# Threshold attention with a feed-forward block: TensorE in program order, feed-forward assigned to the next batch's blocks, two score buffers in the first batch, weights from SyncE's queue

## The chip, the cores and the metric

One core of one Trainium2 chip. The metric is the device time of one execution in microseconds (us), median of several runs. The program uses a single core, so there is no second die to look at; runs of a kernel agree within 0.1 to 0.7% here.

## The reference, cut to what matters

```python
# 8 batches, 8 heads, 576 tokens, head size 64, all float32 (weights come as float64)
scores = (q @ k.T) / 8
scores = where(scores >= max(scores) - tau, scores, -1e9)     # tau = 0.02
attn   = exp(scores - max(scores)); attn /= attn.sum() + 1e-9
x      = (attn @ v) with heads side by side      # 4608 tokens x 512
out    = relu(x @ w_in)**2 @ w_out               # 512 -> 2048 -> 512
```

## The kernel before

Two heads of 64 form a pair that fills the 128 rows of TensorE: 4 pairs per batch, 32 in all. A pair has five blocks of queries (four of 128 rows, one of 64). Each block goes through scores (TensorE), maximum (VectorE), exponential (ScalarE), mask with row sums (VectorE), nine transposes (TensorE; five in the block of 64). After its last block a pair's values are multiplied and divided by the sums. The feed-forward runs on 18 pieces of 256 tokens: 8 hidden groups of 8 matmuls of 256 columns, then 2 x 16 output matmuls of 512 columns.

PSUM has eight banks. One score tile takes four, and four single banks serve everything else:

```python
sc = ps.tile([P, 4 * BANK], FP32, tag="sc", bufs=1, name="sc")     # one score buffer
def bank(shape, name): return ps.tile(shape, FP32, tag="b", name=name)   # bufs=4
```

The feed-forward is cut into units that the loop over blocks hands out evenly; the scheduler may reorder each engine's instructions:

```python
per_slot = NPIECE * 16 / len(slots)
for n in range(len(slots) + 1):
    if n < len(slots): sc = scores(*slots[n])
    if n > 0:          transposes(*slots[n - 1])
    if n < len(slots): softmax(*slots[n], sc)
    ...                                        # cut: next pair's q and k, values
    weights_until(min(2 * (n + 1), len(chunks)))
    credit = run(credit + per_slot) if todo else 0.0
```

In the first batch it takes two blocks of all four pairs first, so that 256 tokens are ready early, and multiplies their values in two halves. Weights are fetched from GpSimd's DMA queue and converted from float64 by ScalarE, VectorE and GpSimd.

## Time and profile before

| | before |
|---|---|
| median of 3 runs | 1737.53 us (1736.78 to 1739.94) |
| span of the profiled run | 1732.0 us, mean granted TensorE clock 0.977 |
| TensorE busy | 1643.5 us, 95% |
| VectorE, ScalarE, GpSimd busy | 33%, 34%, 16% |

TensorE is the bound, and its few holes lie in the first 90 us and around 300 to 370 us. The lines, and how each is read, stand in the prediction. One more view: what TensorE waited for, with the total in us, how often, and the longest wait.

```profile
PE pwT L258 <- DVE w L237: 41.7, 14, 5.0
PE sc L211 <- DVE w L237: 14.6, 7, 2.4
```

Transposes waiting for the mask, 42 us in 14 waits, are the largest item in the whole run of 1732 us.

### The profile page before, as it was taken

Reading aid. Unit: us, or ns where it says so; the run is one execution under the profiler, and the core shown is the slowest. Engines: PE = TensorE matmul, PEld = TensorE weight load, DVE = VectorE, ACT = ScalarE, POOL = GpSimd, SP = SyncE. Lnnn points to the kernel's source line nnn. Section 1 sums busy time; section 2 is a strip of 40 time slices with the busy share of each in tenths; the row PEclk is TensorE's granted clock in tenths of the full one; section 3 lists DMA queues with packets and bytes.
Section 4 is the critical chain, followed back from the end, with each engine's and each line's share of the span. In section 5 each row is a group of like instructions: output and inputs, shape, how many; then the busy total and the mean of one; then the engine's idle time right before and its main releaser. Section 6 shows DMA issues by size and latency. Waiting matters only on the chain.

```text
span 1732.0 us, 19750 instructions
## 1 busy us (share of the span) xinstructions
PE 1643.5 (95%) x7720; PEld 1038.6 (60%) x7720; DVE 569.2 (33%) x1218; ACT 581.8 (34%) x1241; POOL 271.4 (16%) x322
## 2 busy tenths in 40 slices
PE   5699899699999999989999999999999999999998
PEld 3474564366564747566666666565756575747764
DVE  4745333433333333333333333333333333320000
ACT  4644333333333323233333333332333332321100
POOL 4654010001010201011011011010101010102210
PEclk9799999889998999999999999999999999999999
DMA  7532101000101010010101010101010000000000
GB/s 197 165 97 81 34 21 33 21 22 22 33 15 33 21 27 16 24 27 21 34 17 30 22 33 7 34 21 34 15 33 21 19 15 13 1 12 0 13 12 12
DMA packets 128108, 56.70 MB, mean 33 GB/s; under 512 B 121616, under 2 KB 121616, under 8 KB 128016
## 3 DMA queue, kind: packets, MB, share of 16 engines
q1 hardware_dynamic: 120528, 29.22, 7.6%
q0 software_dynamic: 7488, 26.22, 4.5%
q8 instruction: 62, 1.02, 0.2%
q14 instruction: 30, 0.25, 0.1%
HBM read 45.97 MB, written 9.44 MB: 32 GB/s over the span
## 4 chain that ended last, share of the span: by engine, by line
PE 87%; ACT 4%; DVE 3%; issue 3%; POOL 2%; DMA 1%; SPq 0%; POOLq 0%; ACTq 0%
PE ph L334 29%; PE po L352 26%; PE sc L211 12%; PE pwT L258 7%; PE pv L291 7%; PE pqk L180 1%; ACT w L233 1%; PE pv L285 1%; DVE w L237 1%; PE pwT L263 1%; PE pr L309 1%; ACT wT L265 1%; PE pwR L268 1%; DVE nmx L225 1%; DVE t L118 1%
## 5 line engine op out<-in xcount | busy, mean ns | idle before, releaser
L334 PE MATMUL ph<-x,w_in 128*128 128x256 f32 x2304 | 514.4, 381 | 4.5 <-ACT rb L310 2.8
L352 PE MATMUL po<-w_out,g 128*128 128x512 f32 x1152 | 510.8, 593 | 1.4 <-POOL w_out L123 1.4
L334 PEld LDWEIGHTS ph<-x,w_in 128*128 128x128 f32 x2304 | 433.2, 190 | 74.0 <-ACT rb L317 9.1
L225 DVE TENSOR_REDUCE nmx<-sc 128x2 f32<-128x1152 f32 (+1 forms) x160 | 197.9, 1237 | 633.8 <-PE sc L211 633.8
L352 PEld LDWEIGHTS po<-w_out,g 128*128 128x128 f32 x1152 | 212.5, 190 | 232.6 <-issue 228.1
L237 DVE SCALAR_TENSOR_TENSOR w<-sc,thr,w 128x576 f32<-128x576 f32 x288 | 225.2, 815 | 186.7 <-ACT w L233 186.6
L211 PE MATMUL sc<-kT,qT 64*128 64x64 f32 (+3 forms) x1280 | 235.7, 466 | 15.7 <-DVE w L237 14.6
L259 ACT COPY wT<-pwT 128x512 f32<-128x512 f32 x256 | 138.8, 588 | 320.8 <-PE pwT L258 320.5
L340 POOL TENSOR_TENSOR g<-h 128x512 f32<-128x512 f32 x144 | 149.7, 1039 | 563.7 <-ACT h L338 563.7
L211 PEld LDWEIGHTS sc<-kT,qT 64*128 64x128 f32 (+1 forms) x1280 | 115.0, 187 | 185.5 <-issue 181.4
L338 ACT ACTIVATE h<-ph 128x512 f32<-128x512 f32 x144 | 86.0, 597 | 363.7 <-PE ph L334 337.6
L233 ACT ACTIVATE w<-sc,nmx 128x576 f32<-128x576 f32 x288 | 202.0, 756 | 8.6 <-DVE nmx L225 7.7
L258 PE MATMUL pwT<-ident,w 128*128 128x128 f32 x1024 | 151.0, 290 | 42.1 <-DVE w L237 41.7
L258 PEld LDWEIGHTS pwT<-ident,w 128*128 128x128 f32 x1024 | 114.1, 145 | 55.1 <-DVE w L237 39.3
L291 PE MATMUL pv<-wT,va 128*64 128x64 f32 (+2 forms) x1088 | 136.9, 400 | 0.0
L357 POOL DMA_DIRECT2D out_dram<-o x36 | 20.2, 561 | 574.0 <-ACT o L356 574.0
L291 PEld LDWEIGHTS pv<-wT,va 128*64 128x64 f32 x1088 | 60.2, 138 | 73.9 <-issue 68.2
L356 ACT COPY o<-po 128x512 f32<-128x512 f32 x36 | 21.1, 585 | 189.3 <-PE po L352 189.3
L302 POOL COPY rx<-rcp 128x512 f32<-128x512 f32 (+1 forms) x36 | 21.6, 600 | 264.7 <-DVE rcp L300 264.7
L325 DVE TENSOR_TENSOR x<-pv,rb 128x64 f32<-128x64 f32 (+3 forms) x120 | 31.3, 312 | 93.5 <-ACT rb L310 93.2
L310 ACT COPY rb<-pr 128x512 f32<-128x512 f32 (+1 forms) x36 | 19.4, 540 | 116.1 <-PE pr L309 116.1
L265 ACT COPY wT<-pwT 128x256 f32<-128x256 f32 x64 | 20.7, 375 | 105.9 <-PE pwT L263 105.9
(47 smaller groups left out, 698.0 us busy)
## 6 DMA issues: line engine op xcount, KB each, us to landing
out_dram<-o POOLq DMA_DIRECT2D x36, 256.0 KB, 2.3
qn<-in_q_dram SPq DMA_DIRECT2D x66, 128.0 KB, 2.5
kn<-in_k_dram SPq DMA_DIRECT2D x66, 128.0 KB, 2.7
va<-in_v_dram SPq DMA_DIRECT2D x66, 128.0 KB, 2.9
raw<-in_moe_w_in_dram POOLq DMA_DIRECT2D x16, 512.0 KB, 5.1
raw<-in_moe_w_out_dram POOLq DMA_DIRECT2D x16, 512.0 KB, 4.2
rn<-in_q_dram SPq DMA_DIRECT2D x66, 16.0 KB, 2.4
rn<-in_k_dram SPq DMA_DIRECT2D x66, 16.0 KB, 2.5
```

Of the source, the lines that this page charges most:

```text
L211: nc.tensor.matmul(to, qT[rows, ds(t * P, m)], kT[rows, ds(k0, n)], start=True, stop=True)
L225: nc.vector.tensor_reduce(out=nmx[:, 0:nj], in_=every, axis=AXIS.X, op=ALU.max, negate=True)
L233: nc.scalar.activation(out=w[:, ts(j, S)], in_=sc[:, ds(at[j], S)], func=AF.Exp, bias=nmx[:, j : j + 1], scale=1.0)
L237: nc.vector.scalar_tensor_tensor(out=w[:, ts(j, S)], in0=sc[:, ds(at[j], S)], scalar=thr[:, j : j + 1], in1=w[:, ts(j, S)], op0=ALU.is_ge, ...
L258: nc.tensor.transpose(pt[:, c, :], w[:, ds(j * (S + REST) + c * P, P)], ident[:, :])
L259: nc.scalar.copy(wT[:, j, :, ts(t, P)], pt[:, :, :])
L265: nc.scalar.copy(wT[:, j, :, rest], pt[:, :, ds(j * REST, REST)])
L291: nc.tensor.matmul(to[rows, :], va[:, c, rows], wT[:, j, c, ds(q0, n)], start=False, stop=(c == FULL - 1), skip_group_check=True,)
L334: nc.tensor.matmul(ph[:, m, :], w_in[:, c, ts(f + m, P)], x[:, c, :], start=(c == 0), stop=(c == NP - 1))
L338: nc.scalar.activation(out=h[:, :, :], in_=ph[:, :, :], func=AF.Relu)
L340: nc.gpsimd.tensor_mul(g[:, :, :], h[:, :, :], h[:, :, :])
L352: nc.tensor.matmul(po[:, :], gT[f][:, ts(s, P)], w_out[:, f, :], start=(f == 0), stop=(f == NF - 1))
```

## The change

Its intent: keep TensorE full with work placed by hand. TensorE's instructions stay in program order. The first batch, which has no feed-forward to mix in, is taken whole with two score buffers of three banks, so that the next block's scores are made before this block's transposes. From the second batch on, the feed-forward of one batch is spread over the twenty blocks of the next, by a budget in us. Smaller parts: the values of the first batch in one piece; the rest keys of a first-batch block as one matmul over a diagonal tile; fewer, larger loads of q, k and v; weights from SyncE's queue, and converted at 1.25 chunks per block, not two.

```diff
-    ps = ctx.enter_context(tc.tile_pool(name="ps", bufs=4, space=...PSUM))
+    def open_psum(stack, n_scores, bufs, n_banks): ...      # cut
-        nc.gpsimd.dma_start(out=raw[:, :], in_=src.bitcast(I32))
+        nc.sync.dma_start(out=raw[:, :], in_=src.bitcast(I32))
...
+    def feed_forward(x, piece):
+        for f in range(0, NF, 2):                 # NF = 16: eight groups
+            for m in range(2):
+                for c in range(NP):               # NP = 4
+                    nc.tensor.matmul(ph[:, m, :], ...)
+                    ... yield 0.44
+        for s in range(PT // P):
+            for f in range(NF):
+                nc.tensor.matmul(po[:, :], ...)
+                ... yield 0.87
+
+    PIECE = 16 * 8 * 0.44 + 2 * 16 * 0.87
...
+    def run(us):
+        while todo and us > 0:
+            step = next(todo[0], None)
+            if step is None: todo.popleft()
+            else: us -= step; asked["us"] -= step
+        return us
+    share = [0.5] + [4.5 / (NB - 1)] * (NB - 1)
...
+    with ExitStack() as stack, tc.manual_schedule(engines={mybir.EngineType.PE}):
+        open_psum(stack, 3, 2, 2)                 # first batch: two score buffers
+        ...                                       # begin(n + 1) before end(n)
+    with ExitStack() as stack, tc.manual_schedule(engines={mybir.EngineType.PE}):
+        open_psum(stack, 4, 1, 4)                 # the others: one
+        late = 0.0
+        for n in range(n_first, len(slots)):
+            convert_for(n)
+            begin(n)                              # scores, softmax, last pair's values
+            if n % n_first == 0: per_slot = asked["us"] / n_first
+            late = run(per_slot * share[t] + late)
+            end(n)                                # transposes
```

More of the change, by code (lines that the diff above doesn't have):

```diff
@@ L55, with open_psum @@
     sb = ctx.enter_context(tc.tile_pool(name="sb", bufs=2))
-    ps = ctx.enter_context(tc.tile_pool(name="ps", bufs=4, space=bass.MemoryType.PSUM))
+    PSUM = bass.MemoryType.PSUM
+    psum = {}
+    def open_psum(stack, n_scores, bufs, n_banks):
+        psum["n"] = n_scores
+        psum["sc"] = stack.enter_context(tc.tile_pool(name=f"sc{n_scores}", bufs=bufs, space=PSUM))
+        psum["b"] = stack.enter_context(tc.tile_pool(name=f"b{n_banks}", bufs=n_banks, space=PSUM))
     def bank(shape, name):
-        return ps.tile(shape, FP32, tag="b", name=name)
+        return psum["b"].tile(shape, FP32, tag="b", name=name)
     ident = const.tile([P, P], FP32, name="ident")
@@ L78 @@
     vdiag = [const.tile([P, P], FP32, name=f"vdiag{i}") for i in range(4)]
-    for t in vdiag:
+    kdiag = [const.tile([P, P], FP32, name=f"kdiag{i}") for i in range(2)]
+    for t in vdiag + kdiag:
         nc.gpsimd.memset(t[:, :], 0.0)
@@ L88, in fetch_weight @@
         if src.dtype == FP32:
-            nc.gpsimd.dma_start(out=dst, in_=src)
+            nc.sync.dma_start(out=dst, in_=src)
             return None
         raw = sb.tile([P, 2 * WC], I32, tag="raw", bufs=3, name="raw")
-        nc.gpsimd.dma_start(out=raw[:, :], in_=src.bitcast(I32))
+        nc.sync.dma_start(out=raw[:, :], in_=src.bitcast(I32))
         return raw
@@ L154, in load @@
         b, hp = pairs[i]
+        h = 2 * hp
         qn = sb.tile([P, FULL, P], FP32, tag="qn", name="qn")
         kn = sb.tile([P, FULL, P], FP32, tag="kn", name="kn")
-        va = sb.tile([P, FULL, P], FP32, tag="va", bufs=4, name="va")
+        va = sb.tile([P, 2, FULL, D], FP32, tag="va", bufs=3, name="va")
         rn = sb.tile([P, P], FP32, tag="rn", name="rn")
         vd = vdiag[i % 4]
-        for src, dst, order, rest in (
-            (q, qn, "(t p) d -> p t d", lambda j: rn[0:REST, ds(j * D, D)]),
-            (k, kn, "(p t) d -> p t d", lambda j: rn[REST:P, ds(j * D, D)]),
-            (v, va, "(p t) d -> p t d", lambda j: vd[ds(j * D, D), ds(j * D, D)]),
-        ):
-            for j in range(2):
-                h = 2 * hp + j
-                nc.sync.dma_start(out=dst[:, :, ds(j * D, D)], in_=src[b, h, 0:MAIN, :].rearrange(order, p=P))
-                nc.sync.dma_start(out=rest(j), in_=src[b, h, MAIN:S, :])
+        for src, dst, order, rows in ((q, qn, "(t p) d -> p t d", 0), (k, kn, "(p t) d -> p t d", REST)):
+            for j in range(2):
+                nc.sync.dma_start(out=dst[:, :, ds(j * D, D)], in_=src[b, h + j, 0:MAIN, :].rearrange(order, p=P))
+            nc.sync.dma_start(
+                out=rn[ds(rows, REST), :].rearrange("p (j d) -> p j d", j=2),
+                in_=src[b, h : h + 2, MAIN:S, :].rearrange("j p d -> p j d"),
+            )
+        nc.sync.dma_start(out=va[:, :, :, :], in_=v[b, h : h + 2, 0:MAIN, :].rearrange("j (p t) d -> p j t d", p=P))
+        for j in range(2):
+            nc.sync.dma_start(out=vd[ds(j * D, D), ds(j * D, D)], in_=v[b, h + j, MAIN:S, :])
         loaded[i] = (qn, kn, rn, va, vd)
@@ L174, in turn @@
         qn, kn, rn, va, vd = loaded.pop(i)
-        qT = sb.tile([P, S], FP32, tag="qT", bufs=4, name="qT")
-        kT = sb.tile([P, S], FP32, tag="kT", bufs=4, name="kT")
+        qT = sb.tile([P, S], FP32, tag="qT", name="qT")
+        kT = sb.tile([P, S], FP32, tag="kT", name="kT")
         for nat, to in ((qn, qT), (kn, kT)):
@@ L189, in turn @@
         nc.scalar.copy(kT[:, MAIN:S], pt[:, REST:P])
+        if pairs[i][0] == 0:
+            for j in range(2):
+                rows = ds(j * D, D)
+                nc.gpsimd.tensor_copy(out=kdiag[i % 2][rows, ds(j * REST, REST)], in_=kT[rows, MAIN:S])
         turned[i] = (qT, kT, va, vd)
@@ L198, in scores @@
         m = BLK[t]
-        sc = ps.tile([P, 4 * BANK], FP32, tag="sc", bufs=1, name="sc")
-        for part in range(2):
+        n_banks = psum["n"]
+        sc = psum["sc"].tile([P, n_banks * BANK], FP32, tag="sc", name="sc")
+        b_main = (n_banks - 1) * BANK
+        one_rest = t < FULL and n_banks == 3
+        for part in range(1 if one_rest else 2):
             for j in range(2):
@@ L209, in scores @@
                 else:
-                    to = sc[:, ds((3 * BANK, 3 * BANK - REST)[part], n)]
+                    to = sc[:, ds((b_main, b_main - REST)[part], n)]
                 nc.tensor.matmul(to, qT[rows, ds(t * P, m)], kT[rows, ds(k0, n)], start=True, stop=True)
+        if one_rest:
+            to = sc[:, MAIN:S]
+            to = bass.AP(tensor=to.tensor, offset=to.offset, ap=[to.ap[0], [b_main - S, 2], [1, REST]])
+            nc.tensor.matmul(to, qT[:, ts(t, P)], kdiag[i % 2][:, :], start=True, stop=True)
         return sc
@@ L216, in softmax @@
         nj = 2 if t < FULL else 1
-        at = (0, 3 * BANK - REST)[0:nj]
+        at = (0, (psum["n"] - 1) * BANK - REST)[0:nj]
         if i not in sums:
@@ L274, in transposes, with values, reciprocals @@
                 nc.scalar.copy(wR[rows, rest], pt[rows, ds(j * REST, REST)])
-    def values(i, t0, t1):
+    def values(i):
         b, hp = pairs[i]
         wT, wR = weights.pop(i)
-        _, _, va, vd = turned[i]
-        nt = min(t1, FULL) - t0
-        parts = [(t0 * P, nt * P)] + ([(MAIN, REST)] if t1 == NB else [])
+        _, _, va, vd = turned.pop(i)
+        sm = sums.pop(i)
+        last = 2 * FULL
+        rcp = sb.tile([P, 2 * NB], FP32, tag="rcp", name="rcp")
+        nc.vector.tensor_scalar(
+            out=rcp[:, 0 : last + 1], in0=sm[:, 0 : last + 1], scalar1=1e-9, scalar2=None, op0=ALU.add
+        )
+        nc.vector.reciprocal(out=rcp[:, 0 : last + 1], in_=rcp[:, 0 : last + 1])
+        rx = sb.tile([P, FULL, 2, D], FP32, tag="rx", bufs=1, name="rx")
+        nc.gpsimd.tensor_copy(
+            out=rx.rearrange("p t j d -> p (t j) d"), in_=rcp[:, 0:last].unsqueeze(2).broadcast_to([P, last, D])
+        )
+        rb = sb.tile([P, S], FP32, tag="rb", name="rb")
+        yield
+        def reciprocals():
+            pr = bank([P, FULL, P], "pr")
+            for t in range(FULL):
+                nc.tensor.transpose(pr[:, t, :], rx[:, t, :, :].rearrange("p j d -> p (j d)"), ident[:, :])
+            nc.scalar.copy(rb[:, 0:MAIN], pr.rearrange("p t m -> p (t m)"))
+            pr = bank([P, P], "prr")
+            nc.tensor.transpose(pr[:, :], rcp[:, last : last + 1].broadcast_to([P, P]), ident[:, :])
+            for j in range(2):
+                rows = ds(j * REST, REST)
+                nc.scalar.copy(rb[rows, MAIN:S], pr[rows, ds(j * REST, REST)])
+        if b == 0:
+            reciprocals()
+        parts = [(0, MAIN), (MAIN, REST)]
         pv = [bank([P, n], "pv") for _, n in parts]
@@ L291, in values @@
                     nc.tensor.matmul(
-                        to[rows, :], va[:, c, rows], wT[:, j, c, ds(q0, n)], start=False, stop=(c == FULL - 1),
+                        to[rows, :], va[:, j, c, :], wT[:, j, c, ds(q0, n)], start=False, stop=(c == FULL - 1),
                         skip_group_check=True,
                     )
-        sm = sums.pop(i)
-        s0, s1 = 2 * t0, min(2 * t1, 2 * FULL + 1)
-        rcp = sb.tile([P, 2 * NB], FP32, tag="rcp", name="rcp")
-        nc.vector.tensor_scalar(out=rcp[:, s0:s1], in0=sm[:, s0:s1], scalar1=1e-9, scalar2=None, op0=ALU.add)
-        nc.vector.reciprocal(out=rcp[:, s0:s1], in_=rcp[:, s0:s1])
-        rx = sb.tile([P, FULL, 2, D], FP32, tag="rx", bufs=1, name="rx")
-        nc.gpsimd.tensor_copy(
-            out=rx[:, 0:nt, :, :].rearrange("p t j d -> p (t j) d"),
-            in_=rcp[:, s0 : s0 + 2 * nt].unsqueeze(2).broadcast_to([P, 2 * nt, D]),
-        )
-        rb = sb.tile([P, S], FP32, tag="rb", name="rb")
-        pr = bank([P, FULL, P], "pr")
-        for t in range(nt):
-            nc.tensor.transpose(pr[:, t, :], rx[:, t, :, :].rearrange("p j d -> p (j d)"), ident[:, :])
-        nc.scalar.copy(rb[:, ds(t0 * P, nt * P)], pr[:, 0:nt, :].rearrange("p t m -> p (t m)"))
-        if t1 == NB:
-            turned.pop(i)
-            pr = bank([P, P], "prr")
-            nc.tensor.transpose(pr[:, :], rcp[:, 2 * FULL : 2 * FULL + 1].broadcast_to([P, P]), ident[:, :])
-            for j in range(2):
-                rows = ds(j * REST, REST)
-                nc.scalar.copy(rb[rows, MAIN:S], pr[rows, ds(j * REST, REST)])
+        if b > 0:
+            reciprocals()
         for (q0, n), to in zip(parts, pv):
@@ L326, in values @@
                 at += step
-    def hidden(x, gT, f):
-        def go():
+    def feed_forward(x, piece):
+        gT = {}
+        for f in range(0, NF, 2):
             weights_until(NP * (f * P // WC + 1))
@@ L336, in go @@
                     )
+                    if (m, c) != (1, NP - 1):
+                        yield 0.44
             h = sb.tile([P, 2, PT], FP32, tag="h", name="h")
@@ L341, in go @@
             gT[f], gT[f + 1] = g[:, 0, :], g[:, 1, :]
-        return go
-    def output(gT, row, s, f0, f1):
-        def go():
-            weights_until(n_in + f1)
-            if f0 == 0:
-                gT[s, "po"] = bank([P, DM], "po")
-            po = gT[s, "po"]
-            for f in range(f0, f1):
+            yield 0.44
+        for s in range(PT // P):
+            po = bank([P, DM], "po")
+            for f in range(NF):
+                weights_until(n_in + f + 1)
                 nc.tensor.matmul(po[:, :], gT[f][:, ts(s, P)], w_out[:, f, :], start=(f == 0), stop=(f == NF - 1))
-            if f1 < NF:
-                return
+                if f < NF - 1:
+                    yield 0.87
             o = sb.tile([P, DM], FP32, tag="o", name="o")
             nc.scalar.copy(o[:, :], po[:, :])
-            nc.gpsimd.dma_start(out=out[ds(row, P), :], in_=o[:, :])
-        return go
+            nc.gpsimd.dma_start(out=out[ds(piece * PT + s * P, P), :], in_=o[:, :])
+            yield 0.87
+    PIECE = 16 * 8 * 0.44 + 2 * 16 * 0.87
     todo = deque()
-    asked = {"pieces": 0}
+    asked = {"pieces": 0, "us": 0.0}
     def feed_forward_until(tokens):
@@ L367, in feed_forward_until @@
             piece = asked["pieces"]
-            x, gT = xs.pop(piece), {}
-            for f in range(0, NF, 2):
-                todo.append(hidden(x, gT, f))
-            for s in range(PT // P):
-                for f in range(0, NF, 4):
-                    todo.append(output(gT, piece * PT + s * P, s, f, f + 4))
-            asked["pieces"] = piece + 1
-    def run(units):
-        while todo and units >= 1:
-            todo.popleft()()
-            units -= 1
-        return units
-    HALF = 2
@@ L384 @@
-    slots = [(i, t) for i in range(NP) for t in range(HALF)]
-    slots += [(i, t) for i in range(NP) for t in range(HALF, NB)]
-    slots += [(i, t) for i in range(NP, len(pairs)) for t in range(NB)]
-    ends = {}
-    for i in range(len(pairs)):
-        if i < NP:
-            ends[i, HALF - 1] = (0, HALF)
-            ends[i, NB - 1] = (HALF, NB)
-        else:
-            ends[i, NB - 1] = (0, NB)
-    per_slot = NPIECE * 16 / len(slots)
-    load(0)
-    load(1)
-    turn(0)
-    weights_until(1)
@@ L400 @@
-    credit = 0.0
-    for n in range(len(slots) + 1):
-        if n < len(slots):
-            sc = scores(*slots[n])
-        if n > 0:
-            transposes(*slots[n - 1])
-        if n < len(slots):
-            softmax(*slots[n], sc)
-            i, t = slots[n]
-            if (t == 0 and i + 1 < NP) or (t == NB - 2 and NP <= i + 1 < len(pairs)):
-                turn(i + 1)
-                if i + 2 < NP or (NP < i + 2 < len(pairs)):
-                    load(i + 2)
-        if n > 0 and slots[n - 1] in ends:
-            i, t = slots[n - 1]
-            values(i, *ends[i, t])
-            if i == 0 and t == NB - 1:
-                load(NP)
-            if i == 1 and t == NB - 1:
-                load(NP + 1)
-            b, hp = pairs[i]
-            if hp == NP - 1:
-                feed_forward_until(b * S + (MAIN if t == NB - 1 else P * HALF) + (REST if t == NB - 1 else 0))
-        weights_until(min(2 * (n + 1), len(chunks)))
-        credit = run(credit + per_slot) if todo else 0.0
@@ L426 @@
-    run(float("inf"))
+            todo.append(feed_forward(xs.pop(piece), piece))
+            asked["pieces"] = piece + 1
+            asked["us"] += PIECE
+    def run(us):
+        while todo and us > 0:
+            step = next(todo[0], None)
+            if step is None:
+                todo.popleft()
+            else:
+                us -= step
+                asked["us"] -= step
+        return us
+    slots = [(i, t) for i in range(len(pairs)) for t in range(NB)]
+    n_first = NP * NB
@@ new lines, with begin, end @@
+    share = [0.5] + [4.5 / (NB - 1)] * (NB - 1)
+    due = deque()
+    def begin(n):
+        i, t = slots[n]
+        softmax(i, t, scores(i, t))
+        if due:
+            for _ in due.popleft():
+                pass
+            b, hp = pairs[i - 1]
+            if hp == NP - 1:
+                feed_forward_until((b + 1) * S)
+        if t == NB - 2 and i + 1 < len(pairs):
+            turn(i + 1)
+            if i + 2 < len(pairs):
+                load(i + 2)
+    def end(n):
+        i, t = slots[n]
+        transposes(i, t)
+        if t == NB - 1:
+            job = values(i)
+            next(job)
+            due.append(job)
@@ new lines, in convert_for @@
+    def convert_for(n):
+        weights_until(min((5 * (n + 1)) // 4, len(chunks)))
+    with ExitStack() as stack, tc.manual_schedule(engines={mybir.EngineType.PE}):
+        open_psum(stack, 3, 2, 2)
+        load(0)
+        load(1)
+        turn(0)
+        begin(0)
+        for n in range(n_first):
+            convert_for(n)
+            if n + 1 < n_first:
+                begin(n + 1)
+            end(n)
[3 more added lines that the diff above has]
+        for n in range(n_first, len(slots)):
+            t = slots[n][1]
+            convert_for(n)
+            begin(n)
+            if n % n_first == 0:
+                per_slot = asked["us"] / n_first
+            late = run(per_slot * share[t] + late)
+            end(n)
+        for _ in due.popleft():
+            pass
+        feed_forward_until(B * S)
+        run(float("inf"))
```

## The prediction

> **What bounds the kernel now.** I read the page first (shares and 40 slices), then the groups by line, then TensorE's own order of time, then the chain of waits around the one stretch where TensorE is not full.
>
> ```profile
> span 1732.0 us, 19750 instructions
> PE 1643.5 (95%) x7720; PEld 1038.6 (60%) x7720; DVE 569.2 (33%) x1218; ACT 581.8 (34%) x1241; POOL 271.4 (16%) x322
> PE   5699899699999999989999999999999999999998
> ...
> PEclk9799999889998999999999999999999999999999
> ...
> L334 PE MATMUL ph<-x,w_in 128*128 128x256 f32 x2304 | 514.4, 381 | 4.5 <-ACT rb L310 2.8
> L352 PE MATMUL po<-w_out,g 128*128 128x512 f32 x1152 | 510.8, 593 | 1.4 <-POOL w_out L123 1.4
> ```
>
> TensorE is busy 95% of the span, and from the tenth slice on nearly without a hole: it is the bound. Each fp32 matmul of the source has two records, so the feed-forward is 514.4 + 510.8 = 1025 us of it, or 57 us for each of the 18 pieces of 256 tokens. The other 618 us are attention: 32 pairs of heads with five blocks each. The scheduler mixes feed-forward into the attention so that TensorE has work while VectorE and ScalarE do the softmax. One stretch shows what a block costs when there is none to mix in, about 300 to 370 us, seventh to ninth slice:
>
> ```profile
> 303.10:346.40 43.30, 28.11 (x151) 16.97 (x152) 20.98 (x45) 16.99 (x37) 0.61 (x1) 0.83 0.09 21
> 1558.80:1602.10 43.30, 43.30 (x165) 31.27 (x165) 0.74 (x4) 5.44 (x10) 8.89 (x9) 1.00 0.00 0
> ```
>
> These are windows: stretch, length, then busy time of TensorE, its weight loads, VectorE, ScalarE, GpSimd, then the granted clock. The attention-only stretch has TensorE busy 28 of 43 us at clock 0.83; the second, feed-forward alone, is 43.3 of 43.3 at 1.00. The chain of waits inside the first, start and length:
>
> ```profile
> 305.50 2.35 PE sc L211 x8
> 307.86 0.02 issue
> 307.88 1.37 DVE nmx L225
> 309.25 0.02 issue
> 309.27 1.38 ACT w L233 x2
> 310.65 0.03 issue
> 310.68 0.84 DVE w L237 x2
> 311.51 0.05 issue
> 311.56 1.12 PE pwT L258 x4
> 312.68 2.21 PE sc L211 x8
> 314.88 0.60 PE pwT L258 x4
> ```
>
> Scores, maximum, exponentials, mask, transposes: one after the other, since there is a single score buffer. From the end of the scores (307.85) to the first transpose (311.56) TensorE stands 3.7 us. A pair takes 34.3 us here (scores starting at 298.98 and at 333.30), the next one 37.3 (to 370.55); hidden under feed-forward it would take about 18.
>
> **What the Trainium skill says.** (1) "TensorE: Matmul & The Clock Gate", Part 1: the clock is halved after a window of 3413 ns with the engine idle and restored after a busy one; windows run freely. The trace agrees: transposes of four records take 1.12 us after the 3.0 us gaps and 0.66 us when warm, scores 2.4 against 1.3, and the returns to full speed (307.8, 314.8, 342.0) lie about whole multiples of 3.41 us apart. A mostly idle window was enough. (2) Same page, Part 2 ("What happens when you issue a matmul"): matmuls stay in program order, only weight loads are pulled ahead. So an exposed wait in TensorE's program order is not filled by the hardware. (3) "Perfetto Trace Analysis", Identifying Performance Opportunities: equal bubbles again and again can mean too little PSUM for the next tile. That is the 3.7 us above. (4) "DMA: Bandwidth & Descriptors", Issuing engines are not separate DMA queues: another issuing engine only saves its own issue time. In the trace the 32 weight issues take 9.6 + 9.4 = 19 us of GpSimd, which is 16% busy.
>
> **The change part by part.** I built the changed kernel (not run) and read TensorE's instruction order, since a fixed order is the main thing here.
>
> 1. *Values of the first four pairs whole instead of in two halves.* Before: 16 source matmuls of 256 columns per pair, 32 records at 19.5 us / 128 = 0.152 us busy each; after: 8 of 512, 16 records at 102.5 / 448 = 0.229. 4.9 against 3.7 us, four pairs: about 5 us less work.
> 2. *Rest keys of the first batch as one matmul of 128 columns over a diagonal tile*: two of 64 wide go, 16 blocks; by 52.0 us / 256 = 0.20 us each, at most 3 us.
> 3. *First batch, two three-bank score buffers.* No feed-forward exists yet. In VectorE's built order each block has maximum 1.36, threshold 0.23, two masks 1.57, and conversions at 0.48 + 0.84 us for 1.25 weight chunks; next block's maximum mostly follows this block's masks. Masks also wait for the exponentials, 1.4 us. I take 5.2 us x 16 = 83; four 64-row blocks at 3.5 = 14; copies and products 7; about 3 us at each of three value products (two spare banks, all taken) = 9; start 16.5 (first maximum was at 17.06 before). Sum 130 us until the second batch starts.
> 4. *Feed-forward "spread over the next batch".* The budget of a piece is 16*8*0.44 + 2*16*0.87 = 84 us. But the loop goes over f in steps of two: 8 groups x 8 matmuls = 64 steps of 0.44, so a piece really spends 28.2 + 27.8 = 56 us. Two pieces therefore end after 112 / 8.4 = 13 to 14 of the 20 blocks, and the unspent budget (56 us) both stays in what is asked and is carried as lateness into the next batch's first block, where it grows. The built order confirms it: second batch, feed-forward in blocks 20 to 33; third, 64 + 32 + 14 matmuls in block 40 and the remainder to 44; from the fourth batch on all pieces at once in blocks 60, 80, 100, 120, 140, and none in the nineteen blocks that follow each. So pairs 7, 9 to 11 and 12 to 31, 24 pairs, run attention alone but for their first block, with one score buffer and TensorE in program order.
> 5. *Cost of such a pair.* Scores end to first transpose 3.73 us (chain above). Transposes cold 1.04 + 1.04 + 0.21 = 2.29, warm 1.23; scores 2.35 and 1.23. In program order the next scores also follow all nine transposes, whereas the scheduler put them after four. Blocks 1 to 4 of a pair: 1.23 + 3.73 + 2.29 = 7.2; mostly cold 2.1 + 3.73 + 2.29 = 8.1; the one that also turns the next pair's q and k, whose three ScalarE copies precede the exponentials in the built order, 2.1 + 4.6 + 1.7 = 8.4; the 64-row one 1.5 + 2.5 + 1.0 = 5.0. Block 0 hides its softmax behind the previous pair's values: scores 1.7, values 1.7 + 4.05, reciprocals 0.7, a bank wait about 0.65, transposes 1.2 = 10. Sum 38.7. Check against the measured 34.3 and 37.3: 2.5 us for the later scores of three or four blocks and 0.65 for the bank: 38 to 39.
> 6. *Weights from SyncE*: frees 19 us of GpSimd, off the path. Worth nothing in the sum.
>
> Sum: first batch 130; feed-forward 1025 (three pieces of it after the last block, as the order shows); 24 pairs x 38.6 = 926; pairs 4, 5, 8 hidden at 19 = 57; pair 6, last block exposed, 22; last values 7; end 7 (last store at 1725.1 of 1732 before). 2174 us span; runs lay 5 us over the span before. I predict **2175 us**, 25% longer.
>
> **Rivals.** (a) *The plan as stated works*, feed-forward evenly spread: 130 + 1025 + 28 x 19 + 14 = 1701 us, 2% faster. Against it: the counts in the built order. (b) *The clock stays full between blocks*: a pair is 6.2 + 6.2 + 6.6 + 4.3 + 9.1 = 32.4, so 2175 - 24 x 6.2 = 2026 us. Against it: 1.12 us transposes after gaps even shorter than 3.7. For it: two gaps of 1.9 and 2.5 us were followed by warm transposes. (c) *Waits for banks in program order* also in the hidden blocks, where the scheduler could slip other matmuls in: about 1 us per pair, 28 us; half is in my 19. (d) *SyncE blocks*: a weight fetch that waits for one of three raw buffers holds up the q and k loads behind it. The first batch would be 150 instead of 130.
>
> **Range and chances.** The first batch is good to 15 us, a pair to 1.5 us, thus 36 us for 24; together some 45, skewed to the fast side by (b). 8 in 10: **2100 to 2235**. Faster by over 2%: 0.02, within 2%: 0.02, slower: 0.96; only a misread order could save it.
>
> **What would show it.** Step 4: TensorE's slices fall to 5 or 6 tenths over most of the span, in five periods with a full burst between, and the wait of transposes for the mask becomes the largest TensorE idle, near 24 x 3 x 3 us; ScalarE and VectorE busy unchanged. Step 5: pairs of 37 to 40 us and a mean clock clearly under 0.977 (cold transposes 1.1 us). Step 3: first feed-forward matmul between 125 and 145 us. Wrong if TensorE stays over 90% busy after the fourth batch, or if block periods are near 6 us.

## The result, and the profile after

The changed kernel is correct and takes 2177.77 us (median of 4 runs, 2172.39 to 2178.35), against 1737.15 us before (4 runs). The ratio is 1.253, with a 95% interval of 1.250 to 1.255.

The page of the changed kernel: span, busy time, and the rows of forty slices (54 us each) for TensorE, VectorE and the granted clock.

```profile
span 2170.6 us, 19420 instructions
PE 1804.5 (83%) x7616; PEld 1133.4 (52%) x7616; DVE 558.7 (26%) x1210; ACT 596.7 (27%) x1237; POOL 254.2 (12%) x296
PE   6789979986799667999667996779966799667998
DVE  6853241124300333000443004330033300343000
PEclk9999988998799667999787996679966799667999
```

Read the three rows together, from the tenth slice on. Where TensorE has a 9, VectorE has a 0: feed-forward alone. Where TensorE has a 6 or 7, VectorE works and the clock is at 6 to 8 tenths: attention alone. The two no longer share a slice. TensorE is busy for longer than before (1804.5 against 1643.5 us) with fewer instructions, which is what a lower clock looks like. VectorE and ScalarE have as much to do as before.

What TensorE waited for, as in the view of before:

```profile
PE pwT L284 <- DVE w L263: 248.6, 85, 3.7
PE pwT L289 <- DVE w L263: 66.7, 29, 2.5
```

Transposes waiting for the mask take 315 us now, where it was 42. The chain of waits in one block without feed-forward (start, length), in the place of the chain shown of before:

```profile
748.54 2.35 PE sc L233 x8
750.89 0.03 issue
750.91 1.37 DVE nmx L251
752.28 0.03 issue
752.31 1.38 ACT w L259 x2
753.69 0.03 issue
753.71 0.84 DVE w L263 x2
754.55 0.04 issue
754.59 1.97 PE pwT L284 x8
756.56 0.21 PE pwR L294
756.77 2.23 PE sc L233 x8
```

It is the same chain; scores 2.35, wait 3.7, transposes 2.18: 8.2 us a block, all of TensorE's part at the low clock. And TensorE in order of time where the fourth batch begins, with the feed-forward of both pieces in one go:

```profile
589.91 27.89 PE L367 MATMUL ph<-x,w_in 128*128 128x256 f32 x128 [0.57 <-ACT rb L325]
617.64 27.63 PE L382 MATMUL po<-w_out,g 128*128 128x512 f32 x64
645.11 27.79 PE L367 MATMUL ph<-x,w_in 128*128 128x256 f32 x128
672.74 27.63 PE L382 MATMUL po<-w_out,g 128*128 128x512 f32 x64
```

A piece takes 645.11 - 589.91 = 55.2 us.

### The profile page after: what moved, and what is told of

Same layout as the page of the kernel before. It is cut to its first block, busy times and chain, and to the rows that moved or that the text cites. A ratio compares the mean times of both kernels' runs of the same rounds, so it can differ in the third digit from the quotient of the medians.

```text
span 2170.6 us, 19420 instructions
## 1 busy us (share of the span) xinstructions
PE 1804.5 (83%) x7616; PEld 1133.4 (52%) x7616; DVE 558.7 (26%) x1210; ACT 596.7 (27%) x1237; POOL 254.2 (12%) x296
## 4 chain that ended last, share of the span: by engine, by line
PE 78%; DVE 9%; ACT 9%; issue 2%; POOL 1%; SPq 1%; DMA 0%; POOLq 0%; ACTq 0%; DVEq 0%
PE ph L367 23%; PE po L382 22%; PE sc L233 13%; PE pwT L284 8%; ACT w L259 6%; PE pv L343 6%; DVE w L263 4%; DVE nmx L251 4%; PE pv L337 3%; PE pwT L289 1%; PE pwR L294 1%; PE pqk L194 1%; PE pr L324 1%; ACT rb L325 1%; ACT qT L197 1%
## 5 line engine op out<-in xcount | busy, mean ns | idle before, releaser
L367 PE MATMUL ph<-x,w_in 128*128 128x256 f32 x2304 | 502.8, 380 | 4.0 <-ACT rb L325 4.0
L382 PE MATMUL po<-w_out,g 128*128 128x512 f32 x1152 | 499.4, 593 | 1.1 <-ACT rb L325 1.1
L284 PE MATMUL pwT<-ident,w 128*128 128x128 f32 x1024 | 198.0, 353 | 267.8 <-DVE w L263 248.6
L284 PEld LDWEIGHTS pwT<-ident,w 128*128 128x128 f32 x1024 | 152.1, 179 | 304.2 <-DVE w L263 261.1
L233 PE MATMUL sc<-kT,qT 64*128 64x512 f32 (+3 forms) x1216 | 302.7, 633 | 0.0
L233 PEld LDWEIGHTS sc<-kT,qT 64*128 64x128 f32 (+1 forms) x1216 | 138.5, 250 | 165.4 <-issue 138.1
L343 PE MATMUL pv<-wT,va 128*64 128x64 f32 (+1 forms) x1024 | 134.2, 415 | 0.0
L316 POOL COPY rx<-rcp 128x512 f32<-128x512 f32 x32 | 19.9, 620 | 900.4 <-DVE rcp L314 786.0
L289 PE MATMUL pwT<-ident,w 128*128 128x128 f32 x128 | 29.7, 374 | 66.7 <-DVE w L263 66.7
L337 PE MATMUL pv<-wR,vdiag 128*128 128x64 f32 (+1 forms) x128 | 64.6, 648 | 2.3 <-ACT rb L325 2.3
L294 PE MATMUL pwR<-ident,w 128*128 128x128 f32 x160 | 57.8, 361 | 6.1 <-ACT wT L285 4.4
```

The source lines that it names most:

```text
L233: nc.tensor.matmul(to, qT[rows, ds(t * P, m)], kT[rows, ds(k0, n)], start=True, stop=True)
L284: nc.tensor.transpose(pt[:, c, :], w[:, ds(j * (S + REST) + c * P, P)], ident[:, :])
L337: nc.tensor.matmul(to[:, :], vd[:, :], wR[:, ds(q0, n)], start=True, stop=False, skip_group_check=True)
L343: nc.tensor.matmul(to[rows, :], va[:, j, c, :], wT[:, j, c, ds(q0, n)], start=False, stop=(c == FULL - 1), skip_group_check=True,)
L367: nc.tensor.matmul(ph[:, m, :], w_in[:, c, ts(f + m, P)], x[:, c, :], start=(c == 0), stop=(c == NP - 1))
L382: nc.tensor.matmul(po[:, :], gT[f][:, ts(s, P)], w_out[:, f, :], start=(f == 0), stop=(f == NF - 1))
```

## The experiments

Theory: the budget of a piece is about 1.5 times what it spends, the surplus is carried on, and so the feed-forward of a batch collapses into a burst at the next batch's first block; the blocks after it expose the chain score to transpose, once each, at the low clock. Rivals: program order itself, or waits for banks in it, cost the time; the clock has no part; the softmax's own work limits these stretches. Eleven kernels ran, all gave correct results.

### The budget put right

```diff
-    PIECE = 16 * 8 * 0.44 + 2 * 16 * 0.87
+    PIECE = 8 * 8 * 0.44 + 2 * 16 * 0.87
```

> The changed kernel with the budget of a piece put right (8 groups of 8 steps in place of 16), so that the feed-forward really spreads over all twenty blocks of the next batch. My theory (the bursts leave the softmax exposed): 24 pairs fall from 38 to 41 us to about 19, about 1700 us, 2% faster than the kernel before, and no transpose waits over 1 us for the mask after the first batch. Rival (program order and bank waits are what costs): still over 1900 us.

Measured: 1665.88 us (4 runs) against 1732.74 before in the same rounds, ratio 0.961 (0.958 to 0.963). One wrong factor is worth 512 us, and without it the change gains 4%. TensorE's slices and some of its waits in this kernel, the two largest first:

```profile
PE   6879999999999999999999999999999999999998
PE po L382 <- ACT rb L325: 7.9, 14, 0.6
PE ph L367 <- ACT rb L325: 5.1, 9, 0.6
PE prr L327 <- ACT rb L325: 3.4, 5, 0.7
PE pwT L284 <- DVE w L263: 2.5, 2, 2.2
```

The waits of transposes for the mask are 2.5 and (in the block of 64) 3.9 us in all, in the place of 315, and from the second batch on there are none. This settles the cause of the whole loss; program order is unchanged here and costs nothing like it. The expected 1700 us was 34 us too high: see "Why the prediction was right".

### What is left over is forgotten, not carried

```diff
             late = run(per_slot * share[t] + late)
+            if not todo:
+                late, asked["us"] = min(late, 0.0), 0.0
```

> The changed kernel with the budget of a piece still twice too high for the hidden half, but what is left over is forgotten when the queue is empty (no lateness carried, nothing left in what was asked). Feed-forward then ends after 14 of 20 blocks in every batch in place of moving to its first block. My theory: one 64-row block and one pair exposed per batch, 7 x 24 us over the even spread, about 1865 us. If the wrong budget alone made the loss, the carry adding nothing: 2175 us.

Measured: 1836.74 us (2 runs). The wrong factor alone, without the carry, costs 1836.7 - 1665.9 = 171 us, 24 us for each of the seven batches; the carry costs the other 341. So the step from "ends after 14 blocks" to "all in the first block" is shown, not only read from the instruction order.

### Idle TensorE time filled with useless matmuls

```diff
+            idle = not todo and t > 0
             late = run(per_slot * share[t] + late)
+            if idle:                      # result never read
+                spare = bank([P, 2, PT], "spare")
+                for _ in range((0, 7, 7, 4, 4)[t]):
+                    nc.tensor.matmul(spare[:, 0, :], w_in[:, 0, 0:P], w_in[:, 1, 0:PT], start=True, stop=True)
```

> The changed kernel with the budget still wrong, and idle-time matmuls of no use (7, 7, 4, 4 of 256 columns, 0.45 us each) between scores and transposes of every block that has no feed-forward, written to a spare bank that nobody reads; the result stays right. If the halved clock after each wait is part of a pair's 38 to 41 us, as I hold: scores fall from 2.4 to 1.3 us, transposes from 2.3 to 1.3, a pair to 32 to 34 us, together about 2000 us, faster although more work is done. If the clock has no part: 2178 us or more.

Measured: 2005.19 us (2 runs), 173 us less than the changed kernel, with 532 matmuls more. The windows of one stretch without feed-forward (length, then busy us of TensorE, weight loads, VectorE, ScalarE, GpSimd, then clock), first in the changed kernel:

```profile
741.30:770.90 29.60, 16.97 (x76) 10.84 (x75) 12.24 (x26) 10.80 (x23) 0.62 (x1) 0.62 0.09 20
```

and in the one with useless matmuls, the same four blocks of a pair:

```profile
710.80:734.80 24.00, 20.95 (x120) 14.86 (x119) 12.24 (x26) 10.62 (x23) 0.05 (x1) 1.00 0.11 25
```

The clock is 1.00 in the place of 0.62, and the four blocks take 24.0 us, not 29.6. TensorE in order of time shows where:

```profile
717.29 1.30 PE L233 MATMUL sc<-kT,qT 64*128 64x512 f32 x8
718.52 3.29 PE L469 MATMUL spare<-w_in 128*128 128x256 f32 x14
722.31 0.66 PE L284 MATMUL pwT<-ident,w 128*128 128x128 f32 x4 [0.51 <-DVE w L263]
```

Scores 1.30 us in the place of 2.40, and gaps of 0.5 us. A pair (first scores at 701.81, the next pair's at 734.79) takes 33.0 us; the changed kernel's pair from 730.14 to 770.87 takes 40.7. So about 7.7 us of a pair are the clock; the wait itself stays.

### Two score buffers where the feed-forward is missing

From the fourth batch on, with the burst left as it is (diff cut):

```diff
-        for n in range(n_first, len(slots)):
+        for n in range(n_first, 3 * n_first):
...
+    with ExitStack() as stack, tc.manual_schedule(engines={mybir.EngineType.PE}):
+        open_psum(stack, 3, 2, 2)
+        begin(3 * n_first)
+        for n in range(3 * n_first, len(slots)):
+            if n + 1 < len(slots):
+                begin(n + 1)
+            run(float("inf"))
+            end(n)
```

The reciprocals are transposed before the values there, as in the first batch, since only two single banks are left. A first version, which ran the burst one block late, deadlocked.

> The changed kernel with the budget still wrong, but from the fourth batch on the first batch's layout, two three-bank score buffers and two spare banks, with the next block's scores issued before this block's transposes; all feed-forward of a batch in one burst as before. If the single score buffer in program order is what makes a pair without feed-forward take 38 to 41 us: twenty pairs fall to about 28 (the first batch took 29 to 31 with weight conversions besides), about 1930 us. If the softmax's own work were the limit: unchanged, about 2175 us.

Measured: 1884.05 us (2 runs), 46 below what I expected; a pair took 25.5 us (scores from 1199.47 to 1225.0). Twenty pairs less some 15 us each are the 294 us won; the clock's 7.7 us a pair are in this, since scores run warm there (four records in 1.13 us). The softmax's own work is not the limit of these stretches; the single buffer with its chain is.

### The bursts, with TensorE's order left to the scheduler

```diff
-    with ExitStack() as stack, tc.manual_schedule(engines={mybir.EngineType.PE}):
+    with ExitStack() as stack:                                # both places
```

> The changed kernel with the budget still wrong and TensorE's order left to the scheduler. Its built order has the same bursts and nearly the same order inside the blocks without feed-forward. If the bursts are the cause: 2150 to 2180 us, the scheduler cannot take back what was asked for first. If program order is the cause: far below, towards 1740 us.

Measured: 2160.18 us (2 runs, 2153.50 and 2166.85), ratio 1.242. The scheduler gets back about 18 us. It does not undo an order of asking; program order falls as a cause of the loss. The mean granted clock is 0.910 here, against 0.863, in profiled runs only 19 us apart, so that mean alone does not price the loss.

### Program order alone, two ways

The corrected kernel with the scheduler back (the same edit as above):

> The kernel with the corrected budget, but TensorE's order left to the scheduler again instead of the order of the program. If program order itself gives part of the 4% that the corrected kernel won over the kernel before: slower than its 1666 us by some per cent. If only the order in which the program asks for work matters (the built order of the two differs in the first batch and in a few places at the values): within 1%, 1650 to 1680 us. I hold the second, with the waits for a bank after the values, about 16 us in all, partly filled by the scheduler.

Measured: 1673.04 us (4 runs, 1668.63 to 1676.34), ratio 0.964 (0.960 to 0.967); the corrected kernel had 1665.88, ratio 0.961 (0.958 to 0.963). It was run on another chip. The intervals overlap: no difference is shown. And the kernel before with program order as the only edit:

```diff
+    with tc.manual_schedule(engines={mybir.EngineType.PE}):
         load(0)
         ...                                       # the whole loop, indented
```

> The kernel before with one part of the change alone: TensorE in program order, nothing else. If program order by itself costs (waits that the scheduler filled): 1750 to 1780 us. If it is of no account, as the version with the corrected budget left to the scheduler suggests (1673 against 1666): 1725 to 1750, same.

Measured: 1752.14 us (4 runs) against 1736.66, ratio 1.009 (1.006 to 1.012): in the written order of the kernel before, it costs 0.9%, at the lower end of the first reading. TensorE's waits there:

```profile
PE sc L211 <- DVE w L237: 62.0, 22, 4.4
PE ph L334 <- ACT rb L310: 9.1, 15, 1.5
PE prr L314 <- ACT rb L310: 8.4, 12, 1.0
```

The kernel before issues the scores of block n ahead of the transposes of block n - 1 with one buffer; in program order it is the scores that wait for the mask, not the transposes. That moves most of this wait rather than adding it: 41.7 + 14.6 = 56.3 us before, 62.0 now. The larger part of the loss is waits for ScalarE's copy of the reciprocals, which gives a bank back: 9.1 + 8.4 us, where they were 2.8 + 0.1. This is rival (c) of the prediction, seen in the kernel before. In the corrected kernel the same kind of wait is 16.4 us in all (7.9, 5.1 and 3.4 above), yet leaving the order to the scheduler did not make it faster.

### Weights from GpSimd's queue again

```diff
-        nc.sync.dma_start(out=raw[:, :], in_=src.bitcast(I32))
+        nc.gpsimd.dma_start(out=raw[:, :], in_=src.bitcast(I32))
```

> The kernel with the corrected budget, weights fetched from GpSimd's queue as in the kernel before. My prediction gave the move to SyncE's queue no worth: same within 0.5%, 1660 to 1675 us. If the move mattered, the first batch (126 us) would be some 10 us longer, since 26 issues of 0.6 us each stand between GpSimd's conversions.

Measured: 1673.33 us (4 runs), ratio 0.964 against 0.961 with SyncE's queue. The second batch's first scores start at 132.6 us, not 126.3. So the move is worth some 6 us, 0.4%: small, within the 0.5% that I allowed, but not the nothing that my sum gave it. (The totals alone would not show 0.4%. The shared-bank kernel below, with SyncE's queue, starts its second batch at 126.6 us.) More than half of it is there before the first scores, which start at 13.05 us, not 9.25. The first transposes of k, in the corrected kernel and in this one:

```profile
6.97 1.08 PE L194 MATMUL pqk<-ident,kn 128*128 128x128 f32 x4 [1.27 <-DMA kn<-in_k_dram]
10.78 1.08 PE L194 MATMUL pqk<-ident,kn 128*128 128x128 f32 x4 [5.15 <-DMA kn<-in_k_dram]
```

GpSimd issues two weight fetches of 512 KB at 2.1 us, before SyncE issues the first loads of k at 3.0 us. Loads of k issued in the first 12 us take a median of 5.1 us to land here, 2.8 us there, and these transposes start 3.8 us later. Later in the batch TensorE waits longer for GpSimd's copy of the reciprocals (7.4 us in all, not 1.7). So most of the 6 us is what the fetches run ahead of, and not the issues between GpSimd's conversions that I had expected.

### One score buffer in the first batch too

```diff
-        open_psum(stack, 3, 2, 2)
+        open_psum(stack, 4, 1, 4)
         ...
-            if n + 1 < n_first:
-                begin(n + 1)
+            begin(n)
             end(n)
```

> The kernel with the corrected budget, but the first batch too with one four-bank score buffer and four spare banks, each block's scores after the last block's transposes. If the exposed pair costs about 40 us as in the changed kernel, the first batch rises from 126 to 165 or 175 us: about 1710 us. If the weight conversions on VectorE and ScalarE already set the first batch's pace: unchanged.

Measured: 1728.22 us (4 runs), ratio 0.996, which gives back nearly all of the gain. The windows of the first batch, up to the second batch's first scores, in this kernel and in the corrected one:

```profile
0.00:189.20 189.20, 104.25 (x493) 64.72 (x493) 99.41 (x194) 88.36 (x176) 57.85 (x78) 0.72 0.39 115
```

```profile
0.00:126.30 126.30, 93.00 (x460) 50.42 (x460) 96.53 (x194) 87.29 (x177) 56.94 (x78) 0.93 0.58 170
```

Nearly the same busy time of VectorE and ScalarE, 63 us longer. I had expected 165 to 175 us for it, by the exposed pair's 40; it took 189. The last two pairs took 39.4 us each, as expected; the first two took 51.2 and 50.4, and the conversions lie in them: VectorE is busy 31.6 and 35.2 us there, 16.3 and 16.4 in the last two, and GpSimd, which converts too, 26.1 and 30.0 us against 1.6 and 0.1. So the surplus is the conversions on the same two engines. Nearly the whole 4% hangs on the first batch with its two score buffers. The edit takes the order of asking and the diagonal tile away along with the second buffer, so the buffer's share alone is not shown.

### Two versions that go further

The first puts the 64 rest columns of the values and the transposed last reciprocal into one bank, so that the feed-forward after the values finds one free:

```diff
-            pr = bank([P, P], "prr")
+            pr = tail[:, REST : REST + P]
...
-        pv = [bank([P, n], "pv") for _, n in parts]
+        pv = [bank([P, MAIN], "pv"), tail[:, 0:REST]]
```

> The kernel with the corrected budget, with the 64 rest columns of the values and the transposed last reciprocal in one PSUM bank, so that the next feed-forward matmul finds a free bank and does not wait for ScalarE's copy of the reciprocals (waits of 7.9, 5.1 and 3.4 us in all there). If those waits are all: 1650 us, 1% faster. If ScalarE then merely delays something else, as the bank is only held elsewhere: 1666 us.

Measured: 1643.06 us (4 runs), ratio 0.947 (0.944 to 0.950). In the corrected kernel the output matmuls started 0.84 us after the last reciprocal transpose began (181.87 to 182.71), here 0.11 (181.88 to 181.99). The three waits sum to 16.4 us, the gain is 23: the waits are counted net of the modelled end of the matmul ahead of them, and by starts a pair is shorter by 0.83 us (46.66 to 45.83, 46.93 to 46.10), which for 28 pairs gives 23.

The second also puts off weight conversions:

```diff
-        weights_until(min((5 * (n + 1)) // 4, len(chunks)))
+        weights_until(min((3 * (n + 1)) // 4 if n < n_first else 15 + (5 * (n + 1 - n_first)) // 2, len(chunks)))
```

> The shared-bank version with the weight conversions put off: 15 of the 32 chunks in the first batch in place of 25, the others at 2.5 per block in the second batch, where VectorE is a third busy. If conversions set the pace of the first batch (10 chunks x 1.3 us on VectorE and 1.36 on ScalarE): the second batch starts some 8 to 13 us earlier, about 1633 us. If the chain of scores, softmax and transposes sets it: unchanged at 1643; and if the feed-forward then waits for weights, slower.

Measured: 1638.49 us (4 runs) against 1736.66, ratio 0.944 (0.942 to 0.947), the fastest here: 5.6% less than the kernel before. The second batch starts at 119.7 us in the place of 126.6, a little under what I expected. By the two traces 1.4 of the 6.9 us are given back in the second batch (186.9 us, not 185.4).

## Why the prediction was right

It said 2175 us; the runs gave 2177.77. The mechanism of the loss (steps 4 and 5) held in every run that tried it. That the number lies 3 us off is luck: two terms of the sum were off by about 31 us each with opposite signs. Its last step was off too: "5 us over the span" compares the median with the span of another, faster run. That profiled run took 1734.12 us over a span of 1732.0, so 2 us, as the changed kernel's did (2172.39 over 2170.6); and 2174 + 5 would have been 2179. Its signs came too: transposes waited 315 us for the mask (216 said), the mean clock was 0.863, the first feed-forward matmul came at 132.7 us (125 to 145 said); TensorE's slices fell to 6 and 7 tenths, not 5 or 6. All measured values are from the changed kernel's trace (starts of scores and of feed-forward on TensorE; its span is 2170.6):

| term | predicted | measured | from |
|---|---|---|---|
| first batch | 130 | 125.7 | first scores of the second batch |
| feed-forward, 18 pieces | 1025 | 994 | 18 x 55.2 |
| 24 pairs without feed-forward | 926 | 958 | 294.65 to 334.01; 465.55 to 579.76; 579.76 to 1991.84 less 11 pieces |
| pairs 4, 5, 6 and 8 | 79 | 80 | 125.67 to 294.65 and 334.01 to 465.55, less 4 pieces |
| last values | 7 | 8 | 1991.84 to 1999.56 |
| end | 7 | 5 | last matmul's end to the span's end |
| sum | 2174 | 2171 | |

Point by point, by its own steps:

- **Steps 1 and 2** (less work in the first batch): matmul records fell from 7720 to 7616, as they should. Their worth was not tried on its own; the first batch did not depend on it, as TensorE has holes there.
- **Step 3** (130 us, conversions and softmax set the pace): 126. The one-buffer run shows that without the second buffer it is 189, and the late-weights run that ten conversions less are worth 7 us. The term is 4 us too long at its start: the first maximum came at 11.9 us, not at 16.5. Most of that is the move of the weights to SyncE's queue, since the corrected kernel has it at 12.1 us with SyncE's queue and at 15.9 with GpSimd's. So this is step 6's error, inside step 3's term.
- **Step 4** (budget wrong, surplus carried, bursts): right, with the number of exposed pairs. Two runs show its halves: 171 us the factor, 341 the carry.
- **Step 5** (38.6 us a pair; its parts sum to 38.7): 39.9 on average (958 / 24). The block cycle of 8.1 was 8.2; the error is in the 64-row block (5.0 against 5.9) and in block 0 (10 against 11.2), where I took the scores and first values matmuls as partly warm and they ran cold: 2.2 to 2.4 us each. Its clock share is shown by the useless matmuls: 33.0 us warm, where rival (b) said 32.4. One reading behind this step was wrong: before, TensorE did not stand for the 3.7 us from the scores' end to the first transpose. It ran the other half of the last block's transposes in them and stood 3.03 us (from 308.5 to 311.56). In the changed kernel, where the transposes come first, it does stand 3.73, as the sum had it.
- **The feed-forward term** failed by 31 us. I took the busy time of the group rows, 514.4 + 510.8 us; the spacing of starts in a long burst gives 55.2 us a piece, 994 in all. The traces part the 31 us in two, if each feed-forward record is counted only up to the start of TensorE's next record: 1010 us in the kernel before, 994 in the changed and 1003 in the corrected one. So 15 us are modelled ends that lie beside the next record's start, and the other 16 are feed-forward that took longer where it is mixed into attention; why it did is not shown. Of the 35 us by which rival (a)'s 1701 missed the 1666 measured, this term is then some 22 (1025 less 1003).
- **Step 6** (SyncE's queue worth nothing) failed by a little: some 6 us by the run with GpSimd's queue, most of it k landing earlier and not the issue time that I had looked at.
- **Rival (c)**, bank waits in program order: real, 23 us in the corrected kernel, where they could be removed. **Rival (d)**, SyncE blocked by weight fetches: no sign of it; TensorE's waits for loads are 4.5 us for the first q and next to nothing after.

What stays open is how the 4% of the corrected kernel divides among its parts: they do not add up. Without two buffers all but 0.4% is gone, yet program order costs the kernel before 0.9% by itself and the corrected one nothing that shows. The parts of steps 1 and 2 and the slower pace of the conversions had no run of their own.

## What to carry to other kernels

When work is handed out by a budget, count the budget's steps from the loop that spends it, and read the built instruction order of the bound engine before any run: here one wrong factor turned an even spread into bursts and a gain of 4% into a loss of 25%. Do not carry unspent budget past an empty queue. A stretch in which one stage is missing shows the chain that it hid, and its price on TensorE is double: the wait, and a slower clock for the work after it.

## What the Trainium skill lacked or had wrong

- "TensorE: Matmul & The Clock Gate", Part 4, says of transpose mode that the full clock does not engage for it. Here eight transposes (`nc.tensor.transpose`, float32) took 1.04 us in warm stretches and 1.97 after a gap, nearly the same ratio as the scores' 1.30 and 2.40. Whether transposes alone would raise the clock, no run shows.
- The same page, Part 1, has the cycle of waits and cold bursts, with bursts of 2 us. It lacks that bursts longer than its window, 4.3 to 5.5 us with gaps of 2.5 to 3.7 us between, stay mostly cold too (0.62 over four blocks), and that matmuls of no use in the gaps can win more than they cost: a pair fell from 40.7 to 33.0 us.
- "Perfetto Trace Analysis", Identifying the Most-Contended Engine, warns that matmul busy time is a poor measure, as pipelined instructions look smaller. It lacks that a group's busy time can also come out too large: 1002 us by groups against 994 by the spacing of starts in the changed kernel, 1025 against 1010 in the kernel before.
- "DMA: Bandwidth & Descriptors", Issuing engines are not separate DMA queues, says that another issuing engine saves issue time alone. It lacks that the queue also decides what a fetch runs ahead of: with the weights on GpSimd's queue the first transposes of k started at 10.78 us, with all on SyncE's at 6.97.
- No page states that a float32 matmul shows as two records in the trace; 128 records of 256 columns took 27.7 us for 64 matmuls of the source. A float32 transpose shows as one.
